# Window attention and SiLU MLP: seven products of quarters for eight in the first MLP product of the last four token groups, and two small pieces of work on other engines

## Chip, cores and metric

One core of a Trainium2 chip. The metric is the device time of one execution in microseconds (us). Of the runs, the median is quoted; the profile is one further execution.

## What is computed

Attention with a window of 128 and a distance bias per head, over 8 batches, 8 heads, 576 positions and 64 dimensions, and behind it an MLP with SiLU over the 4608 tokens of 512 features. All is float32.

```
scores = where(mask, (q @ k.T) / 8 - slope_h * |i - j|, -1e9);  mask: 0 <= i - j < 128
attn   = exp(scores - max);  attn /= sum(attn) + 1e-9
x      = (attn @ v), heads side by side                # 4608 x 512
h      = x @ w_in                                       # 512 x 2048
out    = (h * sigmoid(h)) @ w_out                       # 2048 x 512
```

To keep float32 accuracy on TensorE (PE), every operand of the MLP is split in a high and a low part, and a product is three matmuls: high by high, high by low, low by high.

## The kernel before

The 4608 tokens are 36 tiles of 128 (`NTILE`), and these are 9 groups of 512 (`NG`, `GT` = 4 tiles). The MLP of group g runs while the attention of the tiles of group g + 1 is done in between. A tile's attention is two pairs p = 2i and 2i + 1 (four heads each): `scores` (L278) writes scores to PSUM, `row_max` (L298, DVE) adds the bias and takes the maximum, `exps` (L308, ACT), `p_hi` and `p_lo` (L317 ACT, L322 DVE) split the weights in fp16 parts, `p_transpose` (L330) turns them by a transposing DMA on SP's queue, `attend` (L368) multiplies by V, and `normalize` (L386 to L395, DVE) writes x. `x_hi` and `x_lo` (L405 ACT, L411 DVE) split x in fp16, and `x_dma` (L434) turns a tile, 1024 columns, by one more transposing DMA. Scores and attention products share the two PSUM banks `a`, so the scores of the next pair wait until `normalize` has read the last.

In a group, `gemm1` (L457) makes h for one of the 16 slices f of 128 hidden features: 12 matmuls of 512 columns (4 slices of the 512 features by 3), in two halves. `act1` to `act4` (L487 tanh on ACT, L492 on DVE, L502 on ACT, L508 on DVE) make the gated value in a high and a low fp16 part, and `gemm2` (L540) adds it into four output banks: 4 token tiles by 3 matmuls of 512 columns, in two halves. The operands of group 0 and 1 are fp32r; from group 2 (`IN16`) the first product and from group 3 (`OUT16`) the second runs on fp16 weights, which `conv1` to `conv3` make. Group 2 alone moves its tokens in two pieces of 256 columns.

The order of the work is written out by hand. A position is one half of `gemm1` or `gemm2`: 64 positions to a group. `at(p)` gives the position at which the scores of pair p stand, `put` files every other step some positions later, `later` does the same from where the program is, and `begin` issues what is filed for a position ahead of that position's matmuls. The order in which the program issues is the order of each engine's queue. The loop at L780 to L814 walks through the groups.

In group 0 the weights come in too. `w_next` (L729) is called at every second position: load (512 KB each), `w_split1` (L570, ACT), `w_shift` and `w_low` (L576 and L581, DVE), `w_hi` (L591, ACT) and `w_lo` (L595, DVE), for `w_in` and `w_out` in turn. V of each pair of batches has a scale of its own: `vscale_reduce` (L151 DVE, or L154 ACT) takes the largest magnitude of nine tiles; the second scale's nine fall into group 0. GpSimd (POOL) does the high part of V (L249) and the low part of the gated value in groups 0 to 2 (L510).

Of the kernel before, what the change touches and what calls it, by code (L numbers as in the profile page):

```python
# [73 lines left out]
def tile_window_attention_then_silu_mlp(ctx, tc, qk, v, w_in, w_out, base8, out):  # L74
# [92 lines left out]
    def vscale_finish(b, stage):  # L167
# [231 lines left out]
    def x_hi(p):  # L399
        i, q = divmod(p, 2)  # L400
        if i < XD:
            return
# [4 lines left out]
    def x_lo(p):
        i, q = divmod(p, 2)
        if i >= XD:
# [26 lines left out]
    def x_send():  # L436
# [3 lines left out]
        for i in [i for i in whole if i // GT <= now[0] + 1]:  # L440
            whole.remove(i)
            x_dma(i)
# [410 lines left out]
```

## Time and profile before

| | |
|---|---|
| runs: median (lowest to highest) of 3 | 987.19 us (985.68 to 987.44) |
| profiled execution: its time / span of its instructions | 983.54 us / 981.8 us |
| PE busy | 943.0 us, 96% of the span, 6572 matmuls |
| DVE busy | 625.8 us, 64% |
| ACT busy | 481.9 us, 49% |
| POOL busy | 100.2 us, 10% |
| first product in fp16 (L474) / second (L540) | 317.8 us busy in 1536 matmuls / 228.4 + 145.6 us busy in 1152 fp16 matmuls |

PE is TensorE's matmuls, PEld its weight loads, which run beside them, DVE is VectorE, ACT ScalarE, POOL GpSimd, and SPq is SyncE's queue, which here issues every DMA. L12 is line 12 of the kernel. A matmul's recorded length includes its way through the array, so that neighbours overlap; what one takes of PE is the distance between starts. The same holds in a smaller degree on the other engines.

### The profile page before, as it was taken

Reading aid. Unit: us, or ns where it says so; the run is one execution under the profiler, and the core shown is the slowest. Engines: PE = TensorE matmul, PEld = TensorE weight load, DVE = VectorE, ACT = ScalarE, POOL = GpSimd, SP = SyncE. Lnnn points to the kernel's source line nnn. Section 1 sums busy time; section 2 is a strip of 40 time slices with the busy share of each in tenths; the row PEclk is TensorE's granted clock in tenths of the full one; section 3 lists DMA queues with packets and bytes.
Section 4 is the critical chain, followed back from the end, with each engine's and each line's share of the span. In section 5 each row is a group of like instructions: output and inputs, shape, how many; then the busy total and the mean of one; then the engine's idle time right before and its main releaser. Section 6 shows DMA issues by size and latency. Waiting matters only on the chain.

```text
span 981.8 us, 17277 instructions
## 1 busy us (share of the span) xinstructions
PE 943.0 (96%) x6572; PEld 581.3 (59%) x6572; DVE 625.8 (64%) x1599; ACT 481.9 (49%) x984; POOL 100.2 (10%) x97
## 2 busy tenths in 40 slices
PE   7878889899998999999999999999999999999998
PEld 6756667677776887654555554555555545554443
DVE  4888999755666887776666665554655565553222
ACT  4656666677444554555454444444544454433222
POOL 3112123122111222100000000000000000000000
PEclk8998999999999999999999999999999999999999
DMA  7258886723324542432364545332433343331001
GB/s 233 80 167 222 225 209 186 183 65 86 71 70 129 119 119 76 119 86 65 87 151 118 119 97 129 87 86 65 130 86 87 86 129 87 65 54 54 1 1 43
DMA packets 201074, 104.94 MB, mean 107 GB/s; under 512 B 168224, under 2 KB 176416, under 8 KB 200992
## 3 DMA queue, kind: packets, MB, share of 16 engines
q1 hardware_dynamic: 200992, 103.84, 41.5%
q8 instruction: 52, 0.85, 0.4%
q14 instruction: 30, 0.25, 0.1%
HBM read 54.00 MB, written 9.44 MB: 65 GB/s over the span
## 4 chain that ended last, share of the span: by engine, by line
PE 78%; DVE 12%; DMA 4%; ACT 3%; issue 2%; SPq 1%; POOL 0%; ACTq 0%; DVEq 0%; POOLq 0%
PE o L540 32%; PE h L474 30%; PE sp L278 6%; PE h L479 4%; PE av L368 4%; DVE wm L581 2%; DVE t L298 1%; DVE wm L576 1%; DMA wr<-w_in 1%; DVE gt L492 1%; DMA wr<-w_out 1%; DVE hr L322 1%; DVE wol L595 1%; DVE v L260 1%; DMA hl<-hr 1%
## 5 line engine op out<-in xcount | busy, mean ns | idle before, releaser
L474 PE MATMUL h<-xt,wi 128*128 128x512 f16 (+1 forms) x1536 | 317.8, 354 | 0.0
L487 ACT ACTIVATE gt<-h,gsc 128x512 f32<-128x512 f32 x112 | 77.0, 688 | 318.5 <-PE h L474 316.4
L540 PE MATMUL o<-wo,gh 128*128 128x512 f16 x768 | 228.4, 379 | 0.0
L474 PEld LDWEIGHTS <-wi 128*128 128x128 f16 x1536 | 143.6, 98 | 130.8 <-issue 2.2
L492 DVE SCALAR_TENSOR_TENSOR gt<-gt,h 128x512 f32<-128x512 f32 x144 | 98.6, 685 | 174.4 <-ACT gt L487 174.1
L540 PE MATMUL o<-wo,gl 128*128 128x512 f16 x384 | 145.6, 379 | 0.0
L540 PEld LDWEIGHTS <-gh 128*128 128x128 f16 x768 | 74.8, 98 | 88.6
L308 ACT ACTIVATE t<-t,mx 128x256 f32<-128x256 f32 (+1 forms) x288 | 121.3, 486 | 8.5 <-DVE mx L298 8.5
L508 DVE SCALAR_TENSOR_TENSOR gl<-gt,gh 128x512 f16<-128x512 f32 x96 | 66.4, 692 | 74.8 <-ACT gh L502 74.7
L298 DVE CUSTOM_DVE_ANT_0 t<-sp,tab 128x256 f32<-128x256 f32 (+1 forms) x288 | 102.2, 402 | 18.3 <-PE sp L278 18.0
L322 DVE SCALAR_TENSOR_TENSOR hr<-t,hr 128x512 f16<-128x512 f32 (+1 forms) x128 | 93.5, 748 | 21.4 <-ACT hr L317 21.4
L510 POOL TENSOR_TENSOR gl<-gt,gh 128x512 fp32r<-128x512 f32 x45 | 62.1, 1379 | 287.4 <-ACT gh L500 230.9
L278 PEld LDWEIGHTS sp<-k,q 64*128 64x128 f32 x1088 | 68.8, 190 | 31.9 <-issue 30.2
L278 PE MATMUL sp<-k,q 64*128 64x128 f32 x1088 | 83.2, 289 | 4.6 <-DVE xs L395 4.1
L502 ACT ACTIVATE gh<-gt 128x512 f16<-128x512 f32 x96 | 60.0, 625 | 47.5 <-DVE gt L492 47.2
L540 PE MATMUL o<-woh,gh 128*128 128x512 f32 x192 | 79.2, 413 | 0.7 <-DVE mx L298 0.4
L368 PE MATMUL av<-v,hl 128*128 128x65 f16 (+1 forms) x1632 | 63.9, 195 | 16.1 <-DVE mx L298 10.7
L368 PEld LDWEIGHTS <-hl 128*128 128x128 f16 x1632 | 59.5, 99 | 32.6 <-issue 20.6
L540 PE MATMUL o<-woh,gl 128*128 128x512 f32 x192 | 76.8, 400 | 1.6 <-POOL gl L510 1.6
L317 ACT ACTIVATE hr<-t 128x512 f16<-128x512 f32 (+1 forms) x128 | 75.8, 598 | 1.1 <-DMA hl<-hr 1.1
L540 PE MATMUL o<-wol,gh 128*128 128x512 f32 x192 | 76.3, 398 | 0.0
L249 POOL TENSOR_SCALAR v<-rv,vsc 128x512 f16<-128x512 f32 x32 | 27.6, 861 | 443.7 <-DMA rv<-v 262.0
(108 smaller groups left out, 977.1 us busy)
## 6 DMA issues: line engine op xcount, KB each, us to landing
q<-qk SPq DMA_DIRECT2D x36, 256.0 KB, 3.0
k<-qk SPq DMA_DIRECT2D x36, 256.0 KB, 3.1
vm<-v SPq DMA_DIRECT2D x36, 256.0 KB, 3.6
out<-ot SPq DMA_DIRECT2D x36, 256.0 KB, 2.3
wr<-w_in SPq DMA_DIRECT2D x16, 512.0 KB, 4.0
wr<-w_out SPq DMA_DIRECT2D x16, 512.0 KB, 3.9
rv<-v SPq DMA_DIRECT2D x32, 256.0 KB, 2.9
hl<-hr SPq DMA_TRANSPOSE x128, 2.8
```

What stands on the lines that cost most here:

```text
L278: nc.tensor.matmul(sp[h][:, u, o], qs[i][rows, 2 * q + u], ks[i - 1 + o][rows, 2 * q + u], start=True, stop=True, skip_group_check=True,)
L298: nc.vector.tensor_tensor_reduce(out=t[:, h, 2 * P - n :], in0=st[p]["sp"][h][:, u, o].rearrange("p o c -> p (o c)"), in1=tab[:, 4 * q + 2 ...
L308: nc.scalar.activation(x, x, AF.Exp, bias=st[p]["mx"][:, 2 * u + h : 2 * u + h + 1], scale=-1.0)
L317: nc.scalar.activation(split_of(p, u, hr)[:, 0], t[:, :, 2 * P - n :], AF.Copy, scale=PSCALE)
L322: nc.vector.scalar_tensor_tensor(out=hr[:, 1], in0=t[:, :, 2 * P - n :], scalar=PSCALE, in1=hr[:, 0], op0=ALU.mult, op1=ALU.subtract)
L368: nc.tensor.matmul(av[:, 2 * u + h, : rhs.shape[-1]], lhs, rhs, start=(n == 0), stop=(n == len(seq) - 1), skip_group_check=True,)
L474: nc.tensor.matmul(o, w[:, wp, cc], x, start=start and k == 0, stop=stop, skip_group_check=True)
L487: nc.scalar.activation(gt, hps[n], AF.Tanh, scale=scale)
L492: nc.vector.scalar_tensor_tensor(out=gt, in0=gt, scalar=1.0, in1=hps[n], op0=ALU.add, op1=ALU.mult)
L508: nc.vector.scalar_tensor_tensor(out=gl, in0=gt, scalar=CUT, in1=gh, op0=ALU.mult, op1=ALU.subtract)
L510: (nc.vector if n % NF == NF - 1 else nc.gpsimd).tensor_sub(gl, gt, f32(gh))
L540: nc.tensor.matmul(ops[ti], a[:, t], w, start=(f == 0 and i == 0), stop=(f == NF - 1 and i == len(seq) - 1), skip_group_check=True,)
```

## The change

From the sixth group on (g = 5 to 8, `SEVEN = 5`) the first product is done as a product of 2 by 2 blocks with seven block products instead of eight (Winograd's form of Strassen's method). The blocks are halves of the 512 tokens by halves of the 512 features for x, and halves of the features by halves of the 2048 hidden features for w_in, so that one step j of eight makes the hidden slices j and j + 8. Four sums of blocks of x (S1 to S4) and four of w_in are made first, in float32, and then split in fp16 parts; products P1 to P7 are 6 matmuls of 256 columns each (2 slices of 128 features by 3). What eight products would have added up in PSUM is now partly added on DVE: per step j one copy of 512 on ACT and one of 256, one addition of 512 and three of 256 on DVE, into float32 tiles in SBUF, from which tanh and the next step read. The second product stays as it is in number and size. Its last step of a group now runs inside the first step of the next group.

```
+SEVEN = 5
+CUT = 2.0**-21                          (scale of the gated value, -25 before)
 at(p):  return STEP * (p - 2 * GT) - LEAD - (4 if p >= 2 * GT * SEVEN else 0)
 attend of the pairs 38, 39:  a = n + (9 if q else 10)          (13 before)
 vscale_reduce:  if b > 1 or (b == 0 and i % 2): DVE   else: ACT    (b > 0 or i % 2 before)
 w_lo:  (nc.gpsimd if which else nc.vector).tensor_sub(...)         (nc.vector before)

+x_sums(i):        4 x gpsimd tensor_add/sub 128x256 f32      (position z + 3, per two tiles)
+x_sums_hi(i, k):  scalar.copy 128x512, k = 0, 1              (z + 5)
+x_sums_lo(i, k):  vector.tensor_sub 128x512, k = 0, 1        (z + 6)
+x_dma7:  per two tiles 5 transposes: 1024 (even tile), 512 (odd tile), 1024 (S2, S4), 512 (S3), 512 (S1)
+w_sum(f, stage), f = 0..7, positions 196 + 15 f + (0, 3, 6, 11, 12):
+    stage 0, 1: 2 x gpsimd tensor_add 128x256;  stage 2: 4 x gpsimd tensor_sub 128x256
+    stage 3: 2 x scalar.copy 128x512;           stage 4: 2 x vector.tensor_sub 128x512

+def product7(out, g, j, name, start=False):
+    for cc in range(2):
+        for k, (wp, xp) in enumerate(((0, 0), (0, 1), (1, 0))):
+            nc.tensor.matmul(out.rearrange("p (t c) -> p t c", t=2), ws[wp], x[:, :, 2 * xp + cc], ...)
+def gemm1_7(g, j, k):
+    if k == 0:   P6 -> a[1] low, P5 -> a[1] high;  u = scalar.copy(a[1])
+    if k == 1:   P1 -> a[0] low, P7 -> a[0] high;  vector u += a[0];  h[1] high = u low + u high
+    if k == 2:   P2 onto a[0] low, P3 onto a[1] high;  vector h[1] low = u low + a[1] high
+                 later: act7 of part 1 (tanh +1, L492's step +2, high and low +3)
+    if k == 3:   P4 onto a[0] high;  vector h[0] high = u low + a[0] high;  scalar h[0] low = a[0] low
+                 later: act7 of part 0 (tanh and L492's step +1, high and low +2)
+def gemm2_7(g, j, k):   half k // 2, part 1 - k % 2: 2 token tiles x 3 matmuls of 512 columns

 the loop, for g >= SEVEN, per j (one = gemm1_7 of j, rest7 = gemm2_7 of the step before):
+    seq += one[:2] + rest7[:2] + [one[2], rest7[2], one[3], rest7[3]]
+    (first j of group 5: one[0], -, one[1], -, one[2], -, one[3], -)
+    after the last j of group 8: gemm2_7 of it, k in (0, 2, 1, 3)
```

The two banks a[0] and a[1] are the two `h` banks, so each step j uses both. How instructions move is seen at three places.

DVE in groups 6 (before) and 5 (after), two slices f, and one step j. gt and gl are the gated value and its low part, h the PSUM bank, hr the attention weights, r and xs (xq) `normalize`, x the low part of x, u and hs the new float32 tiles. Before:
```order
L492 SCALAR_TENSOR_TENSOR gt_8929<-gt_8929,h_8907 128x512
L260 SCALAR_TENSOR_TENSOR v_68<-rv_8742,vsc_6962,v_67 128x512
L508 SCALAR_TENSOR_TENSOR gl_8950<-gt_8929,gh_8949 128x512
L322 SCALAR_TENSOR_TENSOR hr_0_8947<-t_0_8916,hr_0_8947 128x512
L322 SCALAR_TENSOR_TENSOR hr_1_8960<-t_1_8932,hr_1_8960 128x512
L386 TENSOR_SCALAR r_9007<-av_8971 128x4
L387 RECIPROCAL r_9007<-r_9007 128x4
L492 SCALAR_TENSOR_TENSOR gt_9005<-gt_9005,h_8964 128x512
L395 TENSOR_TENSOR xs_9019<-av_8971,r_9007 128x256
L508 SCALAR_TENSOR_TENSOR gl_9022<-gt_9005,gh_9021 128x512
L411 TENSOR_TENSOR x_9031<-xs_9019,x_9031 128x256
```
After (L586 is L508's step, L578 L492's, L327 L322's, L404 L395's, L428 L411's):
```order
L586 SCALAR_TENSOR_TENSOR gl_5_8225<-gt_5_0_8228,gh_5_8224 128x512
L552 TENSOR_TENSOR u_6_8258<-u_6_8258,h_5_6_0_8244 128x512
L553 TENSOR_TENSOR hs_6_1_8277<-u_6_8258 128x256
L327 SCALAR_TENSOR_TENSOR hr_0_8262<-t_0_8221,hr_0_8262 128x512
L327 SCALAR_TENSOR_TENSOR hr_1_8281<-t_1_8237,hr_1_8281 128x512
L389 TENSOR_SCALAR r_8313<-av_8291,unit_7175 128x4
L392 RECIPROCAL r_8313<-r_8313 128x4
L559 TENSOR_TENSOR hs_6_1_8277<-u_6_8258,h_5_6_1_8245 128x256
L404 TENSOR_TENSOR xq_7899<-av_8291,r_8313 128x256
L428 TENSOR_TENSOR x_8338<-xq_7899,x_8338 128x256
L578 SCALAR_TENSOR_TENSOR gt_6_1_8330<-gt_6_1_8330,hs_6_1_8277 128x512
L565 TENSOR_TENSOR hs_6_0_8276<-u_6_8258,h_5_6_0_8244 128x256
```
L552, L553, L559 and L565 are new, two of them between the attention's steps; L404, whose end the next scores wait for, stands behind L559, which needs the third quarter of the first product (k = 2).

POOL in group 0: v is the high part of V, gl the low part of the gated value. Before:
```order
L249 TENSOR_SCALAR v_67<-rv_1319,vsc_276 128x8x64
L510 TENSOR_TENSOR gl_1669<-gt_1634,gh_1668 128x512
L510 TENSOR_TENSOR gl_1765<-gt_1737,gh_1764 128x512
L510 TENSOR_TENSOR gl_1870<-gt_1822,gh_1869 128x512
L249 TENSOR_SCALAR v_67<-rv_1606,vsc_276 128x8x64
L510 TENSOR_TENSOR gl_1938<-gt_1920,gh_1937 128x512
L510 TENSOR_TENSOR gl_2022<-gt_1999,gh_2021 128x512
L510 TENSOR_TENSOR gl_2134<-gt_2075,gh_2133 128x512
```
After (L702 is L510's step, L254 L249's):
```order
L787 TENSOR_TENSOR wol_100<-wm_1_1514,woh_99 128x512
L702 TENSOR_TENSOR gl_1585<-gt_1535,gh_1584 128x512
L254 TENSOR_SCALAR v_67<-rv_1319,vsc_276 128x8x64
L787 TENSOR_TENSOR wol_104<-wm_1_1616,woh_103 128x512
L702 TENSOR_TENSOR gl_1669<-gt_1634,gh_1668 128x512
L787 TENSOR_TENSOR wol_108<-wm_1_1695,woh_107 128x512
L702 TENSOR_TENSOR gl_1765<-gt_1737,gh_1764 128x512
L787 TENSOR_TENSOR wol_112<-wm_1_1802,woh_111 128x512
```
Between two gl stands now a wol, the low part of a slice of w_out, which DVE had.

SP's queue at the end of a group, where the last two tiles of the next group are turned: hl are attention weights, xt (xq, A, S) the tokens. Before:
```order
L330 DMA_TRANSPOSE hl_0_8024<-hr_0_8009 128x8x128
L330 DMA_TRANSPOSE hl_1_8047<-hr_1_8022 128x8x128
L434 DMA_TRANSPOSE xt_7331<-x_7963 128x8x128
L240 DMA q_8103<-qk 128x512
L236 DMA k_8105<-qk 128x512
L330 DMA_TRANSPOSE hl_0_8146<-hr_0_8135 128x8x128
```
After, two tiles end in four transposes where there was one:
```order
L335 DMA_TRANSPOSE hl_1_8305<-hr_1_8281 128x8x128
L474 DMA_TRANSPOSE A_6_7438<-x_8338 128x4x128
L245 DMA q_8369<-qk 128x512
L241 DMA k_8371<-qk 128x512
L335 DMA_TRANSPOSE hl_0_8440<-hr_0_8417 128x8x128
L479 DMA_TRANSPOSE xq_6_7437<-xsum_0_8410 128x8x128
L481 DMA_TRANSPOSE S_6_7439<-xsum_1_8412 128x4x128
L481 DMA_TRANSPOSE S_6_7440<-xsum_1_8412 128x4x128
L335 DMA_TRANSPOSE hl_1_8477<-hr_1_8438 128x8x128
```
The sums S2 and S4 (L479), S3 and S1 (L481) now stand between the two hl of a pair, and S1 is the last of them; the next group's first position reads S2 and S1.

## Rows read from the trace of the kernel before

**Rows 1.** The busy time of each engine in stretches of the run, all on core 0. Columns: start:end and length in us, then busy us and number of instructions of PE, PEld, DVE, ACT and POOL, then the granted clock of PE as a share of 2.4 GHz, the busy share of the DMA engines and GB/s. 62 to 188 is nearly all of group 0, 296 to 406 is group 2, and the five after it are groups 3 to 7.
```profile
62.00:125.00 63.00, 54.42 (x346) 42.24 (x345) 57.69 (x130) 39.80 (x79) 15.31 (x11) 0.92 0.83 214
125.00:188.00 63.00, 56.62 (x376) 43.91 (x377) 57.42 (x131) 40.19 (x77) 13.74 (x10) 0.97 0.72 187
...
296.00:406.00 110.00, 104.89 (x900) 86.01 (x899) 86.27 (x195) 54.10 (x106) 23.28 (x19) 0.98 0.44 108
406.00:504.00 98.00, 97.81 (x668) 49.34 (x667) 68.37 (x179) 50.60 (x102) 2.78 (x4) 1.00 0.35 92
504.00:603.70 99.70, 98.93 (x708) 50.54 (x707) 63.84 (x183) 44.91 (x91) 3.48 (x4) 1.00 0.53 120
603.70:702.00 98.30, 98.11 (x671) 49.40 (x670) 54.35 (x154) 43.55 (x91) 2.78 (x4) 1.00 0.37 94
702.00:801.00 99.00, 98.81 (x708) 50.52 (x706) 57.16 (x162) 45.05 (x90) 2.78 (x4) 1.00 0.40 97
801.00:892.00 91.00, 91.00 (x630) 46.04 (x629) 47.05 (x127) 38.55 (x76) 2.09 (x3) 1.00 0.33 76
```

**Rows 2.** Who waited for whom, PE's waits alone, in the stretches 62 to 125, 125 to 188 and (two rows) 296 to 406. Columns: us in total, times, the longest in us.
```profile
PE av L368 <- DVE mx L298: 6.5, 3, 2.9
PE av L368 <- DVE mx L298: 4.3, 4, 2.3
PE sp L278 <- DVE xs L395: 3.5, 1, 3.5
PE vs L192 <- DVE vcol L189: 1.1, 1, 1.1
```

**Rows 3.** Instructions of PE in order of time in group 7, equal neighbours merged. Columns: start us, length us, line, operation, tiles, shape, count. The difference of two starts is what a piece takes of PE.
```profile
863.55 1.16 PE L278 MATMUL sp<-k,q 64*128 64x128 f32 x16
864.65 2.76 PE L474 MATMUL h<-xt,wi 128*128 128x512 f16 x12
867.25 0.59 PE L540 MATMUL o<-wo,gh 128*128 128x512 f16 x2
...
871.13 0.89 PE L368 MATMUL av<-v,hl 128*128 128x65 f16 x24
871.86 1.46 PE L474 MATMUL h<-xt,wi 128*128 128x512 f16 x6
```

**Rows 4.** The same view in group 2, the only place where the first product moves 256 columns at a time.
```profile
318.35 2.79 PE L474 MATMUL h<-xt,wi 128*128 128x256 f16 x24
320.90 0.48 PE L540 MATMUL o<-woh,gh 128*128 128x512 f32 x1
```

**Rows 5.** The weight loads of the same piece, in the view of PE's weight loads in order of time.
```profile
318.35 2.52 PEld L474 LDWEIGHTS <-wi 128*128 128x128 f16 x24
```

**Rows 6.** Groups of instructions on DVE from 406 to 982 us, by line and shape. Columns: line, engine, operation, tiles, shapes, count | busy us, mean ns of one | idle before them and what ended it.
```profile
L508 DVE SCALAR_TENSOR_TENSOR gl<-gt,gh 128x512 f16<-128x512 f32 x96 | 66.4, 692 | 74.8 <-ACT gh L502 74.7
L492 DVE SCALAR_TENSOR_TENSOR gt<-gt,h 128x512 f32<-128x512 f32 x96 | 65.9, 686 | 147.4 <-ACT gt L487 147.4
...
L322 DVE SCALAR_TENSOR_TENSOR hr<-t,hr 128x512 f16<-128x512 f32 x69 | 45.2, 684 | 1.5 <-ACT hr L317 1.5
L411 DVE TENSOR_TENSOR x<-xs,x 128x256 f16<-128x256 f32 x40 | 16.8, 419 | 6.9 <-ACT x L405 6.9
L395 DVE TENSOR_TENSOR xs<-av,r 128x256 f32<-128x256 f32 x40 | 16.7, 418 | 0.2
```

**Rows 7.** Groups of instructions on ACT, the whole run, same columns.
```profile
L487 ACT ACTIVATE gt<-h,gsc 128x512 f32<-128x512 f32 x112 | 77.0, 688 | 318.5 <-PE h L474 316.4 <-issue 2.1
...
L502 ACT ACTIVATE gh<-gt 128x512 f16<-128x512 f32 x96 | 60.0, 625 | 47.5 <-DVE gt L492 47.2
...
L405 ACT CAST x<-xs 128x256 f16<-128x256 f32 x64 | 25.2, 393 | 3.0 <-DVE xs L395 3.0
...
L154 ACT ACTIVATE vj<-vm 128x512 f32<-128x512 f32 x5 | 3.1, 626 | 2.6 <-DMA vm<-v 2.6
```

**Rows 8.** Groups of instructions on POOL, the whole run, same columns.
```profile
L510 POOL TENSOR_TENSOR gl<-gt,gh 128x512 fp32r<-128x512 f32 x45 | 62.1, 1379 | 287.4 <-ACT gh L500 230.9 <-issue 19.0 <-PE av L368 14.1
```

**Rows 9.** The instructions of line 411 (the low part of x, two inputs in SBUF) in two stretches: first 188 to 296, where POOL works, then 406 to 982, where it hardly does. Columns: duration in ns min/median/max, first and last start, shapes.
```profile
L411 DVE TENSOR_TENSOR x<-xs,x x8: 426/1318/1381, 192.8 to 284.8; 128x256 f16<-128x256 f32 x8
L411 DVE TENSOR_TENSOR x<-xs,x x40: 415/418/426, 410.3 to 887.2; 128x256 f16<-128x256 f32 x40
```

**Rows 10.** Groups of instructions on DVE from 62 to 188 us, by line and shape, columns as in rows 6.
```profile
L595 DVE TENSOR_TENSOR wol<-wm,woh 128x512 fp32r<-128x512 f32 x15 | 13.4, 896 | 0.0
...
L595 DVE TENSOR_TENSOR wil<-wm,wih 128x512 fp32r<-128x512 f32 x14 | 9.5, 682 | 0.7 <-ACT wih L591 0.7
...
L151 DVE TENSOR_REDUCE vmx<-vm 128x1 f32<-128x512 f32 x8 | 5.4, 677 | 0.0
```

**Rows 11.** Instructions of DVE in order of time from 62 to 188 us: the first and the last of the 14 that take 1.3 us or more there; all have one or two inputs in SBUF, and an instruction of POOL runs beside each.
```profile
62.74 1.67 DVE L581 SCALAR_TENSOR_TENSOR wm<-wr,wm 128x512 int32<-128x512 int32 x1
...
176.87 1.78 DVE L581 SCALAR_TENSOR_TENSOR wm<-wr,wm 128x512 int32<-128x512 int32 x1
```

**Rows 12.** The transposing DMAs on SP's queue, of the tokens (L434) and of the attention weights (L330, of 512 or 1024 columns). Columns: issue time in ns min/median/max, first and last start; the line between is L434's time from issue to landing.
```profile
L434 SPq DMA_TRANSPOSE xt<-x x32: 1231/1233/2374, 177.3 to 887.7; - x32
...
DMA to landing us min/median/max: 2.7/2.8/4.0
L330 SPq DMA_TRANSPOSE hl<-hr x128: 1189/1233/2370, 65.7 to 873.7; - x128
```

More of the change, by code (lines that the diff above doesn't have):

```diff
@@ new lines, in tile_window_attention_then_silu_mlp @@
+    w7, banks, u7, h7 = {}, {}, {}, {}
+    def product7(out, g, j, name, start=False):
+        piece, w = {
+            "P1": ("A11", (0, 0)), "P2": ("A12", (0, 2)), "P3": ("S4", (NP7, 2)), "P4": ("A22", (1, 0)),
+            "P5": ("S1", (0, 0, 0)), "P6": ("S2", (1, 1, 0)), "P7": ("S3", (0, 1, 0)),
+        }[name]
+        x = pieces[g][piece]
+        for cc in range(2):
+            if name in ("P1", "P2", "P3"):
+                ws = [w16[0, j + w[0]][:, part, w[1] + cc] for part in range(2)]
+            else:
+                ws = [w7[j][w[0]][:, w[1], part, cc * P : (cc + 1) * P] for part in range(2)]
+            for k, (wp, xp) in enumerate(((0, 0), (0, 1), (1, 0))):
+                nc.tensor.matmul(
+                    out.rearrange("p (t c) -> p t c", t=2), ws[wp], x[:, :, 2 * xp + cc],
+                    start=start and cc == k == 0, stop=cc == 1 and k == 2, skip_group_check=True,
+                )
@@ new lines, in gemm2_7 @@
+    def gemm2_7(g, j, k):
+        half, part = k // 2, 1 - k % 2
+        for ti in (2 * half, 2 * half + 1):
+            if j == 0 and part:
+                ops[ti] = psum.tile([P, DM], F32, tag="wxyz"[ti], name=f"o{g}_{ti}")
+            gh, gl = (t[:, part] for t in gact[g, j])
+            w = w16[1, j + NP7 * part]
+            t = slice(ti % 2 * Q4 + ti // 2 * P, ti % 2 * Q4 + ti // 2 * P + P)
+            for i, (a, wp) in enumerate(((gh, 0), (gh, 1), (gl, 0))):
+                nc.tensor.matmul(
+                    ops[ti], a[:, t], w[:, wp], start=j == 0 and part == 1 and i == 0,
+                    stop=j == NP7 - 1 and part == 0 and i == 2, skip_group_check=True,
+                )
+        if j == NP7 - 1 and part == 0:
+            store(g, 2 * half)
+            store(g, 2 * half + 1)
@@ L439, in x_send @@
             return
[L440 to L442 removed]
+        for a in [a for a in whole if (a[0] if isinstance(a, tuple) else a) // GT <= now[0] + 1]:
+            whole.remove(a)
+            if isinstance(a, tuple):
+                x_dma7(*a)
+            else:
+                x_dma(a)
     def x_parts(i, part):
@@ L681, in tile_window_attention_then_silu_mlp @@
         put(z + 2, x_lo, p)
+        if i // GT >= SEVEN and q and i % 2:
+            put(z + 3, x_sums, i)
+            for k in range(2):
+                put(z + 5, x_sums_hi, i, k)
+                put(z + 6, x_sums_lo, i, k)
         if q == 0:
```

172 lines of the change are left out of this document (165 added, 7 removed).

## The prediction, made before the changed kernel ran

> **What bounds the kernel now.** I read first the busy time by stretch [rows 1]. From 406 to 892 us, groups 3 to 7, PE is busy 98 to 100% of each stretch at the full clock of 2.4 GHz, while DVE is busy 52 to 70% and POOL almost idle: there PE alone sets the pace, and matmul time saved is time saved as long as nothing else becomes late. Group 0, 62 to 188, is another case: DVE is busy 115.1 of 126 us (91%), PE 111.0, so PE stands 15.0 us. PE's waits [rows 2] name 10.8 of these: the attention products wait for DVE's row maxima (seven waits, 2.9 us at most), that is, for a DVE that lags. In group 2 (296 to 406), DVE is at 78% with POOL at work beside it, and PE still stands only 5.1 us, 3.5 of them in one wait that comes once; this is the best likeness for what follows.
>
> **The change, part by part.** The sum is made against the profiled execution (983.54 us; span 981.8); the median of the runs shown is 987.19, 3.65 more, and I carry the difference over.
>
> *a. Seven products for eight.* Per step j (two slices), 24 matmuls of 512 columns become 42 of 256. Twelve of 512 take 867.25 - 864.65 = 2.60 us [rows 3], so 24 take 5.20, and seven eighths of it 4.55: 0.65 saved. Twenty-four of 256 took 320.90 - 318.35 = 2.55 us [rows 4], 0.106 each, so 42 take 4.46: 0.74 saved. There are 32 steps (8 in 4 groups): 20.8 or 23.7 us. I take 20.8, since the neighbours of the second piece are fp32 and its ends are less sure; 19 to 23.7 is the range. The second product keeps its 768 matmuls.
>
> Whether 256 columns are enough to cover a weight load is shown: 24 weight loads, one per matmul, were over in 2.52 us beside them [rows 5]. The Trainium skill (TensorE: Matmul & The Clock Gate, The mechanism) says that a weight load overlaps matmuls in flight only where its row group differs, which speaks against shorter matmuls with more loads; by that rule this piece would have been longer than its matmuls (what that makes of the time is near rival 4), and here the trace does not agree.
>
> *b. Group 0.* DVE loses 15 subtractions for `w_out` (L595, 0.68 us each as for w_in: 10.2) and 8 maxima (L151, 5.4) [rows 10], 15.6 in all. ACT gets nine sweeps of 0.63 (L154) [rows 7], 5.7 us on an engine busy 80 of 126 [rows 1]: hidden. POOL gets 16 subtractions of 1.38 (as L510) [rows 8], 22 us on an engine busy 29 of 126; its own time is hidden, but not what it does to DVE. Where POOL works, the low part of x takes 1.32 us at the median against 0.42 where it doesn't [rows 9], and in this stretch 14 DVE instructions took about 1.0 us longer than the 0.69 that such a one takes elsewhere [rows 6, 11], for 15 subtractions on POOL. So 15 more cost DVE about 14. What is left of the relief is 1.6 us; I take 1.5 saved. The bounds: all waits for the row maxima go (10.8 saved), or DVE's net load rises and a gl queued behind a wol that waits for ACT comes late (POOL's 22 us less the 15.6: 6 lost).
>
> The Trainium skill (SBUF — State Buffer, Who interferes with whom) states this as a rule: a DVE instruction with two inputs in SBUF and a GpSimd instruction that reads SBUF shut each other out for a whole instruction. The trace agrees in kind: 1.32 for 0.42 is most of POOL's 1.3 us. By the rule alone a wol could cost DVE up to 1.38, 21 us in all, and part b would lose 5.
>
> *c. Sums of w_in (groups 3 and 4).* POOL gets 64 instructions of 256 columns, estimated at half of 1.38, 44 us; ACT 16 copies, DVE 16 subtractions (11 us). DVE stands at 132 of 198 us there [rows 1]. With half of POOL's 64 catching a DVE instruction for 0.35 us (11) it comes to 154, 78%, what group 2 had at 1.6 us of small waits. Hidden; 0, at worst 3 lost.
>
> *d. DVE in groups 5 to 7.* A step j adds one addition of 512 (0.69) and three of 256 (0.42 each) [rows 6], 1.95 us, 15.6 per group, the split sums 2.8 less 0.8 for a quarter not split any more, and the sums on POOL (8 per group) block perhaps 3: some 20 on top of 47 to 57 [rows 1], so 75 of about 93 (80%), group 2's level. ACT gets 8 x (0.69 + 0.39) + 2, about 11 on 45 [rows 7]: hidden. Now place by place. A step on PE is, in this order, k = 0 and k = 1 (12 matmuls of 256 each, 1.3), half of the step before's second product (2.6) with an attention product (0.7) in it, k = 2 (1.3), a quarter of the second product (1.3), scores (1.1), k = 3 (6 matmuls, 0.65), and the last quarter (1.3): 11.5 us [rows 3, 4].
> First, k = 2 waits for DVE's addition into u. After k = 1 PE has 3.3 us of other work; DVE needs 0.69 and first has V's low part (0.69, as any of 512) and a lag of up to 1: about 1 us to spare. Second, the second product reads part 0's low part 1.3 + 2.6 + 1.3 + 0.7 = 5.9 us after k = 3; the chain is 0.42 on DVE, tanh 0.69, 0.69, high part 0.63, low part 0.69 [rows 6, 7], with row maxima between: about 4.6, 1 us to spare. Third, the next scores wait for `normalize` (L395), which stands behind L559: 2 x 0.42 and two handings-over after k = 2, against 1.3: 0.2 to spare. Where DVE splits the sums of x (2 x 0.69, two steps per group) this is gone and POOL's blocking comes on top: I take 0.5 us for each of six steps, 3 lost; 0 to 9.
>
> *e. Group starts.* The two last tiles end in four transposes instead of one. A transpose takes SP 1.23 us also with half the columns (L330, 1.19 at least), and lands 2.8 after issue [rows 12]. S1 is third in the row, so it lands 2.5 us later than a first one, and P5, from the seventh matmul of a group on, reads it. Counted from the end of k = 3 a step before: u is added at 5.9, the sums are split by 7.5, the attention weights' low part by 8.1 (DVE); then hl 1.25, S2 with S4 and S3 2.5, S1's landing 2.8: 14.6. PE comes to P5 after 1.3 + 11.5 + 0.65 = 13.4. So 1.2 us late; I take 1.3. At group 5 a start without second product also leaves u's 0.69 to be waited for in part. Four starts: 5 lost; 0 to 10.
>
> The end of the kernel stays: the chain behind the last k = 3 (about 4) runs beside 1.3 + 2.6 us of matmuls; 0.
>
> Sum: -20.8 - 1.5 + 0 + 3 + 5 = -14.3: 969.2 for a run like the profiled one, 972.9 for the median. I say 973.
>
> **The rivals.**
> 1. *DVE becomes the pace in groups 5 to 7: slower.* In group 0 DVE at 91% let PE work 111 of 126 us. The same ratio over the 272 us of PE work left in groups 5 to 7 (98.1 + 98.8 + 91.0 less 15.6 [rows 1]) adds 37 us; without d's 3, 973 - 3 + 37 = 1007. It decides from 0.87 us of standing per step (20.8 over 24 steps), for which DVE must need 12.4 us per step where I count 9.4. For it: DVE takes its work strictly in turn and now waits on PE four times per step; against it: 78% in group 2. 7%.
> 2. *Group 0 comes free.* The 10.8 us of waits go instead of 1.5, since PE no longer lags and the clock (0.92 and 0.97 there [rows 1]) rises: 973 + 1.5 - 10.8 = 964. Against it: POOL's collisions. 17%.
> 3. *POOL's hold on DVE is worse than in the row.* Group 0 loses 6 and c loses 3: 973 + 1.5 + 6 + 3 = 984. For it: from 188 to 296 most low parts of x are hit [rows 9]. 13%. The Trainium skill's page SBUF — State Buffer (Who interferes with whom) is on this side.
> 4. *The change does not do what it says,* that is, 256 columns with ever new weights run slower. At 0.2 us each, twice what rows 4 show, a step's 42 matmuls take 8.4 us, not 4.46: 32 x 3.9 = 126 us more, 1099. Rows 4 and 5 speak against it. 1%.
>
> **How the numbers follow.** My forecast, 967 to 980 by itself, has 62%. The range reaches to rival 2 with part a near its better end and e at nothing (959), and to rival 3 and a little over (985): 959 to 985; rival 1 and the far ends of d and e are left out. A measurement of this kernel can tell about 0.2%, 2 us, from no change. Slower by over that (above 989.2): rival 1 and rival 4, with a piece for d and e at their far ends: 8%. Within it (985.2 to 989.2): 5%, from rival 3 and the far ends. Faster: 87%.
>
> **What would show it.** Right: steps of 11.5 us on PE in groups 5 to 7 (12.2 before by the same sum with 5.2 for 4.5), 9.7 in group 8, PE still at 96% or more, waits of about 1 us at a group's first matmuls for the transpose of S1, DVE at 75 to 82% there; in group 0 no row of L595 for `w_out` on DVE, but as many long rows beside POOL as before or more, up to twice as many, and a length within 3 us of 126. Wrong: PE waits at P2 for line 552 or at the scores for line 404 in most steps (rival 1); group 0 shorter than 120 us (rival 2) or longer than 129 (rival 3); a matmul of 256 columns at more than 0.11 us.

## The result, and the profile after

| | before | after |
|---|---|---|
| runs: median (lowest to highest) of 4 each, on the same chip | 986.43 us (985.63 to 987.44) | 992.94 us (992.18 to 993.72) |
| ratio, 95% interval | | 1.0070 (1.0053 to 1.0088) |
| profiled execution: time / span | 983.54 / 981.8 us | 993.24 / 991.4 us |
| PE / DVE / ACT / POOL busy | 943.0 / 625.8 / 481.9 / 100.2 us | 936.0 / 704.8 / 526.2 / 204.1 us |

In runs 5, 9 and 13 below, one execution each lay far above the rest (1326, 1546 and 1880 us): the medians given there count it, the ratios do not.

The change is 0.7% slower (about 7 us) where 13 us faster was forecast. The miss, some 20 us, is first given a place. The starts of each group's last output instruction on ACT cut the span into groups (us, worked out from those starts; the kernels without sums come below):

| | to the end of group 2 | group 3 | group 4 | groups 5 to 8 |
|---|---|---|---|---|
| before | 405.9 | 97.5 | 99.9 | 374.1 |
| after | 409.8 | 104.2 | 111.0 | 361.9 |
| after without the sums of w_in | 410.6 | 100.7 | 101.9 | 360.6 |
| after without the sums of w_in and x | 408.1 | 100.7 | 100.0 | 357.3 |

The 3.9 us to the end of group 2 say little: in the traces of runs 1 and 4 to 10, whose program is the change's up to there, group 2 ends anywhere from 408.1 to 411.4 us, and the profiled execution of the kernel before is quicker than its four runs (run 2 measures that part). Groups 5 to 8, where the seven products run, are 12.2 us shorter: terms a, d and e together had said 12.8. Groups 3 and 4, in which the sums of w_in are made and of which the sum said 0, are 17.8 us longer.

The windows of the changed kernel, in the columns of [rows 1]; the third and fourth are groups 3 and 4:
```profile
62.00:125.00 63.00, 52.97 (x339) 40.95 (x338) 49.69 (x110) 41.02 (x86) 23.20 (x16) 0.92 0.76 204
125.00:188.00 63.00, 56.05 (x363) 43.11 (x362) 56.42 (x124) 42.75 (x86) 26.70 (x19) 1.00 0.73 194
...
409.70:513.90 104.20, 100.67 (x682) 51.41 (x681) 81.37 (x192) 54.75 (x110) 30.39 (x38) 1.00 0.39 97
513.90:624.90 111.00, 105.04 (x709) 53.35 (x708) 74.46 (x194) 50.75 (x101) 26.01 (x35) 0.95 0.47 110
624.90:720.00 95.10, 91.60 (x814) 63.97 (x813) 70.56 (x192) 53.20 (x113) 10.85 (x12) 1.00 0.42 105
720.00:817.00 97.00, 94.83 (x851) 64.89 (x850) 74.23 (x196) 53.23 (x110) 11.79 (x12) 1.00 0.45 107
817.00:906.00 89.00, 88.70 (x774) 60.86 (x772) 63.28 (x152) 44.80 (x90) 10.63 (x11) 1.00 0.35 81
```
DVE's load is what was forecast: 155.8 us in groups 3 and 4 (154 forecast), 71 to 77% in groups 5 to 7 (75 to 82%). But the group that lost most, group 4, has DVE at only 67% (it would be 75% of the 99.9 us that the group took before). PE stands 6.0 us there, and its busy time is 6 us above [rows 1] too; the granted clock is 0.95.

Who waited for whom, PE's waits alone (total, times, longest): 62 to 188 us, then 409.8 to 624.9, then 624.9 to the end.
```profile
PE av L373 <- DVE mx L303: 10.0, 7, 2.8
PE sp L283 <- DVE xs L404: 2.9, 2, 2.4
...
PE sp L283 <- DVE xq L404: 6.7, 3, 3.4
PE sp L283 <- DVE xs L404: 2.7, 3, 1.6
...
PE h L529 <- DMA S<-xsum: 1.6, 3, 0.7
PE h L529 <- DVE u L552: 1.3, 1, 1.3
PE h L529 <- DMA xq<-xsum: 1.2, 1, 1.2
PE av L373 <- DVE v L265: 0.8, 1, 0.8
PE sp L283 <- DVE xq L404: 0.5, 1, 0.5
```
In groups 3 and 4 the scores wait 9.4 us for `normalize` (L404); in the kernel before there were 1.0 us of waits in this stretch, none of them for `normalize`. At the starts of groups 5 to 8 PE waits 5.4 us (5 were forecast), 4.1 of them for S2, S1 and u (L552) as the forecast had it, and no scores wait in groups 5 to 7 after the first step.

The longest wait, read on three engines. DVE from 555.9 us on (start, length, what; in brackets its idle time before and what ended it):
```profile
555.86 1.22 DVE L700 SCALAR_TENSOR_TENSOR gl<-gt,gh 128x512 f16<-128x512 f32 x1 [1.99 <-ACT gh L694]
557.00 2.35 DVE L455 TENSOR_TENSOR xsum<-xq,xsum 128x512 f16<-128x512 f32 x2
559.27 1.28 DVE L327 SCALAR_TENSOR_TENSOR hr<-t,hr 128x512 f16<-128x512 f32 x2
560.48 0.68 DVE L513 TENSOR_TENSOR w_woh<-wq_woh,w_woh 128x512 f16<-128x512 f32 x1
561.08 0.68 DVE L513 TENSOR_TENSOR w_wol<-wq_wol,w_wol 128x512 f16<-128x512 f32 x1
...
561.96 0.65 DVE L156 TENSOR_REDUCE vmx<-vm 128x1 f32<-128x512 f32 x1
562.53 0.68 DVE L684 SCALAR_TENSOR_TENSOR gt<-gt,h 128x512 f32<-128x512 f32 x1
563.12 0.42 DVE L404 TENSOR_TENSOR xq<-av,r 128x256 f32<-128x256 f32 x1
```
ACT and POOL in the same time:
```profile
552.85 1.13 ACT L451 CAST xsum<-xq 128x512 f16<-128x512 f32 x2
553.88 0.91 ACT L313 ACTIVATE t<-t,mx 128x256 f32<-128x256 f32 x2
...
555.21 0.62 ACT L694 ACTIVATE gh<-gt 128x512 f16<-128x512 f32 x1
...
556.61 1.05 POOL L503 TENSOR_TENSOR wq_wol<-wq_wol,wq_woh 128x256 f32<-128x256 f32 x1
557.74 1.06 POOL L504 TENSOR_TENSOR wq_wol<-wq_wol 128x256 f32<-128x256 f32 x1
```
And PE:
```profile
559.80 0.49 PE L283 MATMUL sp<-k,q 64*128 64x128 f32 x2
563.68 0.58 PE L283 MATMUL sp<-k,q 64*128 64x128 f32 x2 [3.40 <-DVE xq L404]
565.66 4.92 PE L666 MATMUL h<-xt,wi 128*128 128x512 f16 x12
570.41 0.59 PE L732 MATMUL o<-wo,gh 128*128 128x512 f16 x2
```
On ACT the copies of the sums of x (L451) stand ahead of `gh`, so gl comes late on DVE, and DVE stands 2 us for it. Then, in the order in which the program issues: gl and the subtractions of the sums of x (L455), 1.2 us each instead of 0.68 while POOL's pieces run beside them, hr, the subtractions of the sums of w_in (L513), a maximum for V's scale (L156), gt, and only then `normalize` (L404). PE stands 3.40 us. Behind that, twelve matmuls of 512 columns take 570.41 - 565.66 = 4.75 us, where [rows 3] have 2.60: PE runs near the lower of its clock's two levels (1.2 and 2.4 GHz).

The new steps themselves are close to the forecast. PE in group 6:
```profile
752.04 0.82 PE L529 MATMUL h<-xq,w_wol 128*128 128x256 f16 x6
...
754.66 0.59 PE L597 MATMUL o<-wo,gh 128*128 128x512 f16 x2
...
763.96 0.82 PE L529 MATMUL h<-xq,w_wol 128*128 128x256 f16 x6
```
The four runs of 6 from 752.04 to 754.66 make 0.109 us per matmul [rows 4: 0.106]; a step is 763.96 - 752.04 = 11.9 us here (11.5 forecast).

### The profile page after: what moved, and what is told of

Read it like the earlier page. It is cut to its first block, busy times and chain, and to the rows that moved or that the text cites. A ratio compares the mean times of both kernels' runs of the same rounds, so it can differ in the third digit from the quotient of the medians.

```text
span 991.4 us, 18855 instructions
## 1 busy us (share of the span) xinstructions
PE 936.0 (94%) x7148; PEld 644.2 (65%) x7148; DVE 704.8 (71%) x1726; ACT 526.2 (53%) x1090; POOL 204.1 (21%) x209
## 4 chain that ended last, share of the span: by engine, by line
PE 70%; DVE 13%; ACT 5%; DMA 5%; issue 3%; SPq 2%; POOL 0%; ACTq 0%; DVEq 0%; POOLq 0%
PE o L732 14%; PE o L597 14%; PE h L529 12%; PE h L666 12%; PE sp L283 7%; PE h L671 6%; PE av L373 4%; DVE hr L327 2%; DMA wr<-w_in 2%; DVE wm L773 1%; ACT t L313 1%; DVE wm L768 1%; DVE t L303 1%; DMA vm<-v 1%; DVE gt L684 1%
## 5 line engine op out<-in xcount | busy, mean ns | idle before, releaser
L666 PE MATMUL h<-xt,wi 128*128 128x256 f16 (+1 forms) x768 | 140.1, 332 | 0.0
L327 DVE SCALAR_TENSOR_TENSOR hr<-t,hr 128x512 f16<-128x512 f32 (+1 forms) x128 | 98.8, 789 | 25.8 <-ACT hr L322 25.5
L283 PE MATMUL sp<-k,q 64*128 64x128 f32 x1088 | 89.4, 294 | 17.3 <-DVE xs L404 9.0
L666 PEld LDWEIGHTS <-wi 128*128 128x128 f16 x768 | 72.2, 100 | 49.2 <-issue 5.4
L702 POOL TENSOR_TENSOR gl<-gt,gh 128x512 fp32r<-128x512 f32 x45 | 62.0, 1378 | 188.1 <-ACT gh L692 149.6
L574 ACT ACTIVATE gt<-hs,gsc 128x512 f32<-128x512 f32 x64 | 45.9, 717 | 102.8 <-DVE hs L559 102.8
L679 ACT ACTIVATE gt<-h,gsc 128x512 f32<-128x512 f32 x48 | 33.0, 688 | 123.9 <-PE h L666 121.8
L597 PE MATMUL o<-wo,gl 128*128 128x512 f16 x256 | 97.0, 379 | 0.1
L684 DVE SCALAR_TENSOR_TENSOR gt<-gt,h 128x512 f32<-128x512 f32 x80 | 54.6, 683 | 51.2 <-ACT gt L679 50.8
L322 ACT ACTIVATE hr<-t 128x512 f16<-128x512 f32 (+1 forms) x128 | 74.3, 599 | 3.2 <-DMA hl<-hr 3.2
L529 PE MATMUL h<-xq,wi 128*128 128x256 f16 x576 | 73.3, 273 | 1.3 <-DVE u L552 1.3
L597 PEld LDWEIGHTS <-gh 128*128 128x128 f16 x512 | 48.5, 98 | 35.7 <-ACT gh L584 0.6
```

Of the source, the lines that this page charges most:

```text
L283: nc.tensor.matmul(sp[h][:, u, o], qs[i][rows, 2 * q + u], ks[i - 1 + o][rows, 2 * q + u], start=True, stop=True, skip_group_check=True,)
L322: nc.scalar.activation(split_of(p, u, hr)[:, 0], t[:, :, 2 * P - n :], AF.Copy, scale=PSCALE)
L327: nc.vector.scalar_tensor_tensor(out=hr[:, 1], in0=t[:, :, 2 * P - n :], scalar=PSCALE, in1=hr[:, 0], op0=ALU.mult, op1=ALU.subtract)
L529: nc.tensor.matmul(out.rearrange("p (t c) -> p t c", t=2), ws[wp], x[:, :, 2 * xp + cc], start=start and cc == k == 0, stop=cc == 1 and k ...
L597: nc.tensor.matmul(ops[ti], a[:, t], w[:, wp], start=j == 0 and part == 1 and i == 0, stop=j == NP7 - 1 and part == 0 and i == 2, skip_gro ...
L666: nc.tensor.matmul(o, w[:, wp, cc], x, start=start and k == 0, stop=stop, skip_group_check=True)
```

## The experiments

Where more than one edit is compared, the ratio to the kernel before, run on the same chip, is turned into microseconds at 986.3 us, with "+" for slower than before. The change stands at +6.9 by its ratio; one such figure is sure to some 1 to 2 us, so a difference of two of them to some 2.

**1. Without the sums of w_in:** the filing of `w_sum` is dropped.
```
-                ws = [w7[j][w[0]][:, w[1], part, cc * P : (cc + 1) * P] for part in range(2)]
+                ws = [w16[0, j][:, part, 2 * w[0] + cc] for part in range(2)]
```


> The changed kernel without the sums of w_in: w_sum is never called, and P4 to P7 read the sixteen-bit parts of w_in as they are, so that the products are as many and as long but the output is another. Theory (the sums' pieces on GpSimd, ScalarE and VectorE stand ahead of `normalize` in VectorE's queue in groups 3 and 4, the scores wait for it, and the two waits of 3.4 and 2.5 us drag the granted clock down): groups 3 and 4 fall back from 213 us to about 198, and the time from 993 to 974 to 980. Rival 1 (it is the attention of pairs 38 and 39 and of group 5 that was pulled ahead by four positions, with the sums of x): groups 3 and 4 keep most of their loss, 986 to 993. Rival 2 (the two small moves in group 0): the same, 988 to 993.

Measured: 980.90 us, ratio 0.9945 (0.9925 to 0.9965), -5.4: the sums of w_in cost 12.3 us. In its trace the scores of groups 3 and 4 wait 3.6 us for `normalize` instead of 9.4, 0.61 at the place shown above instead of 3.40, and the granted clock of group 4 is 1.00. The time lies just outside the theory's 974 to 980: the sums of w_in are the largest part of the loss, but not all of it; the table above shows 5.2 us left in groups 3 and 4.

**2. The kernel before with the two small moves; 3. the change without them.** The two lines of the diff, done and undone.

> The kernel before with nothing but the two small moves: the low parts of w_out on GpSimd and the second scale of V on ScalarE. The recorded prediction: 1.5 us faster than before (985 against 986.4). Theory now, from the trace of the changed kernel, where group 0 is 1.5 us longer: 0 to 2 us slower, 986 to 989. Its rival that group 0 comes free: 976 to 979. Its rival that the hold on VectorE is worse: 990 to 993.

> The changed kernel with the two small moves undone: seven products alone. If the small moves cost 1.5 us as the trace reads, 991 to 992; if they gain 1.5 by themselves, 994 to 995; if they are what makes the change lose, 975 to 980.

Measured: 987.53, 1.0008 (0.9996 to 1.0020), and 993.49, 1.0068 (1.0046 to 1.0090). Group 0 neither comes free nor is worse: the small moves are worth 0.8 us lost by the one and nothing by the other, neither to be told from no change, and don't explain the result.

**4. The sums of w_in placed elsewhere.**
```
-        for k, n in enumerate((0, 3, 6, 11, 12)):
-            put(SUMS + 15 * f + n, w_sum, f, k)
+        for k, n in enumerate((-22, -18, -14, -5, 0)):
+            put(241 + 16 * f + n, w_sum, f, k)
```


> The changed kernel with the sums of w_in placed elsewhere and else the same: 16 positions apart instead of 15, from 219 to 353 instead of 196 to 313, so that the last stage (VectorE) always comes right behind the row maxima of a pair and the copies (ScalarE) five positions earlier, the last three of them in group 5. Theory (it is the place in the queue, not the amount of work): groups 3 and 4 lose 3 us or less against the kernel before instead of 15, and the time is 975 to 981. Rival (the amount of work on VectorE with GpSimd's hold on it): the loss stays and is only shared with group 5, 987 to 993.

Measured: 991.20, 1.0048 (1.0034 to 1.0062): 2 us, which the intervals can hardly tell from none, far from the 12 to 18 expected. The longest wait for `normalize` is still 3.2 us. The trace says why. POOL in order of time, in the step with sums of x; the pieces of L496 to L503 had been filed at three positions, 8 from first to last, some 13 us by the 104 to 111 us that 64 positions take:
```profile
550.60 0.70 POOL L253 TENSOR_SCALAR v<-rv,vsc 128x512 f16<-128x512 f32 x1
551.26 0.67 POOL L496 TENSOR_TENSOR wq_woh<-wi 128x256 f32<-128x256 f16 x1
...
554.23 0.73 POOL L500 TENSOR_TENSOR wq_woh<-wq_woh 128x256 f32<-128x256 f32 x1
...
556.98 1.05 POOL L503 TENSOR_TENSOR wq_wol<-wq_wol 128x256 f32<-128x256 f32 x1
```
Filing a step at a position gives its place in the queue, not a time. Nothing that POOL's pieces wait for is late, so all eight run in one burst as soon as POOL is free, behind the sums of x, and again beside gl and xsum: 26 of the 64 pieces take 1.0 us or more, 21 in the change.

**5. Only POOL's half of the sums; 6. only the copies and subtractions.**
```
5: -  for k, n in enumerate((0, 3, 6, 11, 12)):     +  for k, n in enumerate((0, 3, 6)):
6: stages 0 to 2 are one gpsimd.memset of each of the two tiles; stages 3 and 4 stay
```


> The changed kernel with only the GpSimd part of the sums of w_in (64 pieces of 256 columns); the copies on ScalarE and the subtractions on VectorE are left out, and P4 to P7 read the sixteen-bit parts as they are, so the output is another. All of w_sum costs 12.0 us (992.9 against 980.9 without it). Theory now (GpSimd's pieces run as soon as GpSimd is free, beside VectorE's subtractions of two inputs, which they make twice as long: 2.34 for two where they meet): this half costs most of it, 7 to 11 us: 988 to 992. Rival (the copies ahead of `gh` on ScalarE and the two subtractions on VectorE): this half costs 1 to 4 us, 982 to 985. No GpSimd piece on its own is on PE's path in either.

> The other half alone: 16 copies on ScalarE and 16 subtractions on VectorE in their places, from two tiles that GpSimd only fills with a constant (no arithmetic on GpSimd, two fills per f); P4 to P7 read the sixteen-bit parts, the output is another. Theory (GpSimd's hold is the larger half): 1 to 5 us over the 980.9 without any of w_sum, 982 to 986. Rival (copies and subtractions): 988 to 992. If the two halves together give less than 12 us, they cost by meeting in the same steps.

Measured: 987.10, 1.0004 (0.9992 to 1.0016), and 987.92, 1.0023 (1.0011 to 1.0036): 5.8 and 7.7 us above the run without either. My theory that POOL's hold is most of it falls: the halves are about equal and add up to the whole within what these figures can tell (13.5 for 12.3), so nothing shows that they cost by meeting. How POOL can hold DVE is seen in the low parts of the sums of x, two of which are long, first in the change, then without the sums of w_in (ns min/median/max):
```profile
L455 DVE TENSOR_TENSOR xsum<-xq,xsum x16: 682/684/1212, 557.0 to 898.9; 128x512 f16<-128x512 f32 x16
...
L455 DVE TENSOR_TENSOR xsum<-xq,xsum x16: 683/684/689, 553.9 to 885.9; 128x512 f16<-128x512 f32 x16
```
The Trainium skill (SBUF — State Buffer, Who interferes with whom) has a DVE instruction with two SBUF inputs and a GpSimd instruction that reads SBUF exclude each other; the trace agrees, 1212 ns for 684.

**7. POOL's pieces held back.** As 4, in five places from -21 to -5 and with the last at 0; ahead of each pair of POOL's pieces DVE writes one column of what they write or read:
```
+            for t in b:
+                nc.vector.memset(t[:, stage, 0:1], 0.0)
```


> The changed kernel with the sums of w_in spread: placed as in the run with late sums, and GpSimd's eight pieces per slice held back in four pairs by a one-column instruction of VectorE ahead of each pair (row maxima of the same step or the normalization's step behind it), so that they no longer run in one burst behind the sums of x. Theory (it is the burst beside xsum, hr and gl that makes `normalize` late): the waits of the scores in groups 3 and 4 fall from 9.3 us to under 5 and the time to 982 to 986, that is, no slower than the kernel before. Rival (the amount of hold, wherever it lies): 988 to 992.

Measured: 988.22, 1.0020 (1.0010 to 1.0030): 4.9 us better than the change, 2 short of the theory's range; groups 3 and 4 take 101.8 + 104.6 us, 206.4 for the change's 215.1. Only 3 of POOL's 64 pieces take 1.0 us or more now, and no low part of the sums of x does.

**8. Neither the sums of w_in nor those of x.** The transposes read the tile's own parts instead.
```
-            put(z + 3, x_sums, i)
...
+            put(z + 6, whole.append, (i, "sums"))
```


> The changed kernel without the sums of w_in and without the sums of x (for S1 to S4 the transposes read the tile's own parts, as many transposes as before; the output is another). Without w_sum alone the time was 980.9, and groups 3 and 4 were still 5.2 us longer than in the kernel before. Theory (the sums of x, two copies ahead of exps and `gh` on ScalarE and four pieces on GpSimd, are what is left of it in group 4, and the late S1 at group starts goes too): 974 to 977. Rival (the attention that was pulled ahead by four positions is what is left, and the starts of the groups wait for u as before): 979 to 981.

Measured: 974.20, 0.9881 (0.9868 to 0.9893), -11.7: the sums of x cost 6.3 us. This kernel has every matmul of the change and comes within some 1 us of the forecast's 973, which is luck: the forecast's sum without d and e gives some 965. By the table the sums of x cost 1.9 us in group 4 and 3.3 in groups 5 to 8. Group 3 is still 3.2 us longer than before, with neither sum: 16 matmuls of scores (1.1 us) stand in it that came later before, and the scores wait twice 0.7 us for `normalize`. The waits of its scores, from 408.1 to 608.7 us and then for the rest of the run, with the other waits there:
```profile
PE sp L283 <- DVE xq L404: 1.5, 2, 0.8
PE sp L283 <- DVE xs L404: 0.7, 1, 0.7
...
PE h L529 <- DVE u L552: 1.3, 1, 1.3
PE av L373 <- DVE v L265: 0.8, 1, 0.8
PE sp L283 <- DVE xq L404: 0.5, 1, 0.5
```

**9. S1 ahead of S3; 10. the same in the gated version.**
```
-        for k, n in enumerate(("S3", "S1")):
+        for k, n in ((1, "S1"), (0, "S3")):
```


> The changed kernel with one edit: of the transposes behind a pair's sums of x, S1 goes ahead of S3. In the changed kernel the first products of groups 6 to 8 stand 0.74, 1.95 and 0.17 us for S2 and S1 (2.9 in all). Theory (S1 is late because it is third in the row of SP's transposes, 1.23 us each): most of the part that is S1's, 1.6 us, goes, and S3 is not waited for: 991 to 992 against 992.9. Rival (it is the sums of x themselves that come late, so that one place in the row does nothing): 993 and the same waits.

> The version with gated sums (988.2) with S1's transposes ahead of S3's, and nothing else. In the changed kernel the same edit took the waits of the group starts away in the trace. Theory: 1.5 to 3 us, 985 to 987; the rest of the way to 981.6 is then the pulled-ahead attention's. Rival: 988.

Measured: 994.29, 1.0095 (1.0062 to 1.0128), and 984.81, 0.9981 (0.9969 to 0.9993). In both traces the waits for S1 are gone, and in 9 groups 5 to 8 take 358.8 us against 361.9. The time of 9 does not show it; its runs scatter from 989.2 to 1003.6 us, so it is 10 that counts: 3.8 us, more than the waits for S1 had shown (2.5 in the trace of 7).

**11. The attention pulled ahead little by little; 12. with S1 first and the gated sums.**
```
-    return STEP * (p - 2 * GT) - LEAD - (4 if p >= 2 * GT * SEVEN else 0)
+    return STEP * (p - 2 * GT) - LEAD - min(max((p - 31) // 2, 0), 4)
...
-        elif 2 * GT * SEVEN - 2 <= p < 2 * GT * SEVEN:  a = n + (9 if q else 10)
+        elif 31 <= p < 39:                              a = n + 12
```


> The changed kernel with the attention pulled ahead over pairs 33 to 39 instead of at pair 40 at once, and nothing else. If that place has a loss of its own (the waits of 1.6 and 0.7 us about 485 and 511 us, and gh late there), 989 to 991; if the work only piles up elsewhere, 992 to 994.

> The run with the gated sums (988.2), with S1 ahead of S3 and the attention pulled ahead by four positions over pairs 33 to 39, one position for every two pairs, instead of all at once at pair 40 (where pairs 38 and 39 were attended to early and the scores of 40 and 41 came right behind `normalize` of 38 and 39). Theory: the waits of 0.8, 1.0 and 0.7 us about 478, 483 and 509 us go, and 1 to 2 us at group starts: 984 to 986, no difference from the kernel before or a little faster. Rival (the waits only move to another pair, since VectorE's work in group 3 is what it is): 987 to 989.

Measured: 991.35, 1.0046 (1.0029 to 1.0064), and 981.61, 0.9955 (0.9942 to 0.9969). By itself the edit gives 2.4 us, though its interval overlaps the change's; on top of 10 it gives 2.6. Both point the same way: the jump by four positions at pair 40 has a loss of its own.

**13. The two waits filled.** Matmuls with zero weights into an open accumulation, ahead of the scores of pairs 46 and 50, else the change as it is.
```
+    def fill(n):
+        for _ in range(n):
+            nc.tensor.matmul(ops[0], zeros, w16[1, 0][:, 0], start=False, stop=False, ...)
+    put(286, fill, 14)
+    put(318, fill, 11)
```


> The changed kernel with 14 matmuls of 512 columns with zero weights into an open accumulation ahead of the scores of pair 46 and 11 ahead of those of pair 50 (3.0 and 2.4 us of PE at 0.216), so that PE works through the two waits of 3.4 and 2.5 us instead of standing. Nothing else moves. In the changed kernel PE's busy time in group 4 is 105.0 us where the run without w_sum has 99.7, with the granted clock at 0.95 of the group. Theory (the clock falls because PE stood): the clock stays at 1.00 behind them, group 4 gets 4 to 6 us shorter and the time is 987 to 990. Rival (the clock falls for another reason, or the fill itself delays what is behind it): 992 to 994.

Measured: 989.08, 1.0024 (1.0012 to 1.0037), 4.5 us better than the change. PE at the same place:
```profile
561.44 3.19 PE L836 MATMUL o<-wo,zeros 128*128 128x512 f16 x14
564.55 0.48 PE L283 MATMUL sp<-k,q 64*128 64x128 f32 x2
565.39 1.13 PE L283 MATMUL sp<-k,q 64*128 64x128 f32 x14 [0.36 <-DVE xq L404]
566.45 2.76 PE L666 MATMUL h<-xt,wi 128*128 128x512 f16 x12
569.05 0.38 PE L732 MATMUL o<-wo,gh 128*128 128x512 f16 x1
```
PE waits as long as before, but at work, and the next twelve matmuls take 569.05 - 566.45 = 2.60 us, not 4.75. The windows behind the wait, first in the change, then here (clock: third number from the end):
```profile
563.70:572.00 8.30, 8.30 (x34) 4.24 (x35) 3.32 (x14) 1.79 (x5) 2.23 (x4) 0.62 0.49 127
...
563.00:572.00 9.00, 8.64 (x50) 4.36 (x49) 5.59 (x19) 3.61 (x8) 0.40 (x1) 1.00 0.71 176
```
Behind the second wait of the change, 2.54 us, the clock is 0.72 over 6.1 us. So some 4.5 us of the change's loss is not waiting but the clock behind two waits.

**14. Group 4's last second products inside group 5's first step; 15. with all sums of w_in 16 positions earlier; 16. as 14 without the sums of w_in.** 14 stands on 12; the code is shortened.
```
 group 4:  + [("g2" if g < SEVEN - 1 else "", n, h) for h in range(2)]        ("" does nothing)
 group 5:  seq += [one[0], last_g2 half 0, one[1], last_g2 half 1, one[2], None, one[3], None]
15: -  put(241 + 16 * f + n, w_sum, f, k)        +  put(225 + 16 * f + n, w_sum, f, k)
```


> The same with group 4's last quarter of the second product (two pieces of 1.3 us with their stores) moved into group 5's first step, between its k = 0, k = 1 and k = 2, which has no second product of its own to cover the addition into u. Theory: the waits at the start of group 5 (u 1.3, scores 0.5, V's low part 0.8 to 1.3 us) fall to under 1 us in all: 982 to 984, faster than the kernel before. Rival: PE waits for the sums' or the stores' work on VectorE instead, 985 or more.

> The same as the last with all of the sums of w_in 16 positions (two pairs' steps) earlier, so that only one of eight slices' sums is left to group 5. Theory (what a slice's sums cost depends on the free time of VectorE in its step, and group 5's steps have less of it, 79 of 99 us busy, than group 4's, 74 of 107): 1 to 2 us faster than the last. Rival (group 3's beginning still has the conversions of w_out): the same or 1 us slower.

> The mended version (980.7) without the sums of w_in (P4 to P7 read the sixteen-bit parts; the output is another): what the sums still cost there. Theory (gated and apart from the sums of x they cost what DVE's tiny pieces and the few waits at V's low part show): 3 us or less, 977 to 980. Rival (they cost 12 us wherever they lie): 969 to 972.

Measured: 980.71, 0.9940 (0.9922 to 0.9958); 980.01, 0.9932 (0.9910 to 0.9953); 976.49, 0.9905 (0.9886 to 0.9924). 14 is 1.5 us better than 12 and 15 0.8 better than 14, both less than these intervals can tell apart. What the sums of w_in cost is down from 12.3 to 3.5 us (16 against 14). Version 15 leaves nothing out and is faster than both kernels, by 0.7% and 1.4%. The four longest of its PE waits from 407.9 us to 970:
```profile
PE sp L282 <- DVE xq L403: 3.5, 4, 1.6
PE h L533 <- DMA xq<-xsum: 1.5, 1, 1.5
PE av L372 <- DVE v L264: 1.3, 1, 1.3
PE vs L196 <- DVE vcol L193: 1.0, 1, 1.0
```

## Why the prediction was wrong

| term | forecast | measured | by |
|---|---|---|---|
| a, seven products | -20.8 | -19.7 | 32 x (5.20 - 42 x 2.62 / 24) |
| b, group 0 | -1.5 | +0.8 | run 2 |
| c, sums of w_in | 0 | +12.3 | run 1 |
| d and e, sums of x, late S1 and the starts | +8 | +8.9 | run 8 (6.3), and the 2.6 us of waits at the start of group 5 that it keeps |
| pulled-ahead attention | not in the sum | +2.4 | run 11 |
| sum | -14.3 | +4.7 | the change: +6.9 |

The rest, some 2 us, is not settled; the errors of five terms are of that size, and the terms were measured in different company (d and e without the sums of w_in, run 11 with them), so the sum is rough.

*a* held: 0.109 us a matmul, so the weight loads are covered (rival 4 is out). *c* is the step that failed: "it comes to 154, 78%, what group 2 had at 1.6 us of small waits. Hidden; 0, at worst 3 lost." The level came true, the conclusion did not. Group 4 with DVE at 67% stood longest, because what PE waits for is not DVE's share but the one instruction `normalize`, and everything that the program issues between an av product and its `normalize` is in front of it. The new work lay there in lumps: two copies of the sums of x on ACT ahead of `gh`, two subtractions of each kind of sum on DVE, eight pieces of POOL in one burst. By the table of groups 3.5 us of c lie in group 3 and 9.1 in group 4, though four of the eight slices' sums are made in each; only in group 4 do the sums of x stand beside them. In the prediction I did ask place by place for groups 5 to 7 (term d) and there the forecast held; for groups 3 and 4 I let a mean answer. In addition, these two waits cost more than their length: 4.5 us of the loss is the clock behind them. [rows 2] held one of that length, 3.5 us, in group 2, whose stretch has a clock of 0.98 in [rows 1]; I read it as a wait of 3.5 us and no more. The trace of the kernel before had the cost to be read behind that wait, a clock of 0.79 over 8.2 us:
```profile
302.80:311.00 8.20, 8.13 (x50) 6.20 (x50) 6.11 (x16) 4.18 (x9) 1.30 (x1) 0.79 0.26 76
```

*b*: DVE was relieved of more than forecast, 9.0 busy us in group 0 (115.1 to 106.1) for 1.6, since its instructions of 1.3 us or more rose from 14 to 17 only, where the term had twice as much hold by POOL; and it bought nothing: the waits for the row maxima fell from 10.8 to 10.0, and the waits for `normalize` rose from 0.7 to 2.9. *d* was near in size, 1.9 us for 3 by run 8, but not in place: the steps with sums of x cost in group 4, where sums of w_in are made too, and behind the first step none of the scores of groups 5 to 7 waits for them. *e* was 5.4 for 5, 4.1 of it by the mechanism named. What the text left out altogether is the line of the diff that moves `at(p)` by four positions for pairs from 40 on; the sum should have had a term for where the two spacings meet.

Of the rivals, 1 had the mechanism (DVE late before the scores) but put it into groups 5 to 7; 3 had the place, "c loses 3", and a quarter of the price.

## What to carry to other kernels

Work added "beside" an engine's load is priced by what stands ahead of the next instruction that the bounding engine waits for, step by step, and not by busy shares: an engine at 67% can be the one that is waited for. Filing an instruction at a later place delays it only if something in its own queue, or an operand, is late; helper work without such a tie runs in a burst, and a one-column instruction can be the tie. Where a wait of PE cannot be removed, matmuls of zeros in it can keep the clock for the work behind, as they did here.

## What the runs showed of the hardware that was not expected

Behind a wait of 3.40 us the granted clock was 0.62 over the next 8.3 us and twelve matmuls took 4.75 us; with 3.19 us of matmuls of zeros in that wait it was 1.00 and 2.60 us. Behind a wait of 2.54 us it was 0.72 over 6.1 us, behind one of 1.64 us (485 us) 1.00. Group 4 as a whole went from 111.0 to 106.2 us when both were filled. POOL's adding or subtracting of two 256-column pieces in SBUF takes 0.67 to 0.73 us alone and some 1.05 beside a DVE instruction of 512 columns with two SBUF inputs, which then takes 1.2 us instead of 0.68; held back by one-column writes of DVE, 3 of 64 such pieces were long instead of 21.
